# An order for every engine, laid out by the kernel itself, in a gated attention and bilinear feed-forward kernel

## The chip, the cores and the metric

The kernel runs on one core of a Trainium2 chip. The metric is the device time of one execution in microseconds (us); the times given are medians of several runs. A core has a matrix engine (PE, with its weight loads shown as PEld), a vector engine (DVE), an activation engine (ACT), GpSimd (POOL), and SP, whose queue issues all transfers of this kernel. The order in which an engine's instructions stand is fixed when the kernel is built; this case is about that order.

## The reference

```
for t in range(S):                       # B=4, H=8, S=768, D=40
    m_new = max(f_gate[t] + m, i_gate[t])
    f_stab = exp(f_gate[t] + m - m_new);  i_stab = exp(i_gate[t] - m_new);  m = m_new
    C = f_stab * C + i_stab * outer(v[t], k[t])
    n = f_stab * n + i_stab * k[t]
    h = C @ q[t];  denom = max(|n . q[t]|, 1)
    y[t] = sigmoid(o_gate[t]) * h / denom
x = y as [3072 tokens, 320]
out = ((x @ w_a) * (x @ w_b)) @ w_out     # w_a, w_b: 320 x 1536; w_out: 1536 x 320
```

All inputs are float32 but the three weights, which come as 64-bit numbers (an 11.8 MB load).

## The kernel before, in words

*Attention.* The recurrence is worked in chunks of 128 steps: 6 chunk rows c by 4 batches b make 24 chunks n, eight heads each. A chunk loads q and k (`qk`, three buffers) and v (`va`, three buffers), forms the masked decay matrix E from the gates (POOL L409, eight exponentials on ACT L416), the scores (`pS`, PE L471, in bf16 pieces that transposing transfers `T<-qks`, L448, have turned), their product with E split in three bf16 pieces (DVE L476, L480, L482, ACT L478), the products with v (`pV`, PE L523) and with the state carried over (`pI`, L497), the state's update (`pU`, L547, and `cst`, `cb`, which go through `c_dram`), and the end: the denominator, the sigmoid of the o gate (`squash`, L167), the products L610 and L613, a copy L615, the transposes `pX` (L633) and the split into a leading and a rest part, `xh` (ACT L637) and `xl` (DVE L639). The o gate of a chunk row has one buffer (`osig`), so its four loads wait for the chunk row before. The pieces q and k are split on DVE at L438 to L445. Chunks 0 to 5 use a plainer form (`begin_...`, L784 to L877).

*Feed-forward.* The 24 chunks are grouped in nine blocks of 2 or 3 (`sizes`). A block runs over twelve column groups ff of 128: two up products of eight matmuls each into `pu` (L747; three buffers in PSUM), then ACT or DVE copies one (`g`, L754), DVE multiplies (L755), a leading part `gh` (L757) and a rest `gl` (L759) are made, and two groups later the down products add into `pd` (L719; one buffer per chunk of the block). `xh` and `xl` have two buffers, so attention may be one block ahead.

*Weights.* They arrive in 32 stages (`fetch`, L331) and are converted once from 64-bit numbers: `high` (ACT L342), `low` (ACT L352), `join` (DVE L357), `lead_part` (ACT L370) and `low_part` (DVE L376).

*What sets the order.* Three means. The prologue (gates, chunks 0 and 1, stages 0 to 4) is written out by hand for PE, ACT, DVE and SP. From then on `run_block` walks a block's matmuls and between them pulls pieces of attention from a generator in a fixed proportion (a letter of `PATTERN` is a piece of a chunk). In blocks 0 and 1 the framework takes this as a priority and orders by its own estimate of time, held back by `issue_after`: nothing is issued ahead of the prologue's last instruction on its engine, and loads keep their order behind the weights. From block 2 on PE and SP keep the order as written, and the framework orders ACT, DVE and POOL:

```
    for kb in range(2):
        run_block(kb)
    with tc.manual_schedule(engines={mybir.EngineType.PE, mybir.EngineType.SP}):
        for kb in range(2, NB):
            run_block(kb)
```

Of the kernel before, what the change touches and what calls it, by code (L numbers as in the profile page):

```python
# [1 line left out]

# [14 lines left out]
PSUM = bass.MemoryType.PSUM  # L17


@with_exitstack  # L20
def kernel(
# [13 lines left out]
    nc = tc.nc  # L35
# [18 lines left out]
    rpool = ctx.enter_context(tc.tile_pool(name="rpool", bufs=1))  # L54
    apool = ctx.enter_context(tc.tile_pool(name="apool", bufs=2))
    dpool = ctx.enter_context(tc.tile_pool(name="dpool", bufs=1, space=bass.MemoryType.DRAM))
    ps_up = ctx.enter_context(tc.tile_pool(name="ps_up", bufs=3, space=PSUM))
    ps_dn = ctx.enter_context(tc.tile_pool(name="ps_dn", bufs=1, space=PSUM))
    ps_at = ctx.enter_context(tc.tile_pool(name="ps_at", bufs=2, space=PSUM))


    ident = wpool.tile([P, P], F32, name="ident")
    make_identity(nc, ident)
    NQ = 3
# [55 lines left out]
    after = {}  # L120
# [4 lines left out]
    issued = {}  # L125
# [12 lines left out]
    def load_qk(n, parts=(0, 1)):  # L138
        c, b = chunks[n]
        for j in parts:  # L140
            x = (q, k)[j]
            issued["qk"[j], n] = nc.sync.dma_start(
                nat(n)[0][:, j, :, 0:D], x[b, :, c * P:(c + 1) * P, :].rearrange("h t d -> t h d")
            ).ins

    def load_v(n):
        c, b = chunks[n]
        issued["v", n] = nc.sync.dma_start(
            nat(n)[1][:, :, 0:D], v[b, :, c * P:(c + 1) * P, :].rearrange("h t d -> t h d")
        ).ins  # L150

    def load(n):
        with tc.issue_after(issued.get(("v", n - 1), issued["w"])):
            load_qk(n)
            load_v(n)
# [9 lines left out]
    def squash(c, b, nb):  # L165
        x = osig[c][:, b:b + nb, 0:DM]
        after["s", c, b] = nc.scalar.activation(x, x, AF.Sigmoid).ins  # L167

    def load_o(c):
        for b in range(B):  # L170
            with tc.issue_after(issued["k", c]):
                fetch_o(c, b)
        squash(c, 0, B)

    def load_g(n):
# [4 lines left out]
        return nc.sync.dma_start(t, g_dram[c:c + 1, b * H:(b + 1) * H, :].broadcast_to([P, H, P])).ins  # L180
# [33 lines left out]
    def later_gates():  # L214
        f, i, m = (x[:, P:] for x in (gf, gi, gm))
        G = tab[0:BH]
        with tc.issue_after(start["dve"]):
            nc.vector.tensor_tensor_scan(m, f, i, gm[:, P - 1:P], op0=ALU.add, op1=ALU.max)
# [5 lines left out]
        with tc.issue_after(start["act"]):  # L224
            nc.scalar.copy(G[:, 0], gb3[0][:, 0])
            nc.scalar.copy(tab[BH:2 * BH, 0], gb3[0][:, 1])
# [7 lines left out]
        with tc.issue_after(issued["w"]):  # L234
            nc.sync.dma_start(g_dram.rearrange("c g t -> g c t"), G)
# [86 lines left out]
    def fetch(x):  # L322
# [6 lines left out]
        with tc.issue_after(issued.get("w", issued["k", 0])):  # L329
            for a in src:  # L330
                raw_in = nc.sync.dma_start(raw[r0:r0 + a.shape[0]], a).ins  # L331
                r0 += a.shape[0]
        issued["w"] = raw_in
# [32 lines left out]
    def lead_part(x):  # L366
        raw, n, W = held[x]
        w = ws[x] = rpool.tile([P, 2, n], F32R, tag=f"s{x}", name=f"w{x}")
        for rows, other, j, jl in parts(x):
            after["act"] = nc.scalar.copy(w[rows, j], W[rows]).ins  # L370

    def low_part(x):
        raw, n, W = held.pop(x)
        w = ws[x]
        for rows, other, j, jl in parts(x):
            after["dve"] = nc.vector.tensor_tensor(  # L376
                w[other, jl], W[rows], w[rows, j].bitcast(F32), op=ALU.subtract
            ).ins

    def weights():  # L380
        for x in range(NF0, len(stages) + 1):
            if x < len(stages):
                with tc.issue_after(start["act"]):
                    high(x)
                    low(x)
                with tc.issue_after(start["dve"]):
                    join(x)
# [206 lines left out]
    def stage_f(n):  # L594
# [10 lines left out]
        after["r", n] = nc.vector.reciprocal(den, den).ins  # L605
# [15 lines left out]
    def stage_d(n):  # L621
# [15 lines left out]
        after["h", n] = nc.scalar.copy(xh[:, :, cols], px).ins  # L637
        yield
        after["x", n] = nc.vector.tensor_tensor(  # L639
            xl[:, :, cols], px, xh[:, :, cols].bitcast(F32), op=ALU.subtract  # L640
        ).ins
# [6 lines left out]
    def aside(o, n):  # L648
        if o == "L" and n + 2 < NCH and n + 2 > NS + 1:
            with tc.issue_after(issued["w"]):  # L650
                load(n + 2)
# [52 lines left out]
    def moe_block(kb):  # L704
# [27 lines left out]
        def up(ff):  # L732
# [5 lines left out]
            for j in range(2):  # L738
# [7 lines left out]
                for x, (a, r) in enumerate(terms):  # L746
                    up_in = nc.tensor.matmul(  # L747
                        acc[j], a, r, start=(x == 0), stop=(x == len(terms) - 1),
                    ).ins
                    start.setdefault("pe", up_in)  # L750
# [21 lines left out]
    def begin_e(n):  # L772
# [5 lines left out]
        first_t = after["t"]  # L778
        for hf in range(2):
            pE = ps_up.tile([P, HH, P], F32, tag="pu", name=f"pE{n}_{hf}")  # L780
            for x in range(HH):
                one_hot = sel[:, b * H + hf * HH + x:b * H + hf * HH + x + 1].broadcast_to([3 * BH, P])
                with tc.issue_after(first_t):
                    nc.tensor.matmul(pE[:, x], one_hot, stk[:, 0], start=True, stop=False)  # L784
# [5 lines left out]
    def begin_a(n):  # L790
# [6 lines left out]
        for j in range(2):  # L797
# [9 lines left out]
            for x in range(HH):  # L807
                after["t"] = nc.tensor.transpose(
                    pt[:, x], nat(n)[0][:, j, 2 * x:2 * x + 2, :].rearrange("t h d -> t (h d)"), ident
                ).ins  # L810
# [71 lines left out]
    def lead(pieces, by):  # L882

        for _ in iter(int, 1):
            with tc.high_priority(by):
                x = next(pieces, "end")
# [5 lines left out]
    cpool = ctx.enter_context(tc.tile_pool(name="cpool", bufs=1))  # L892
    mpool = ctx.enter_context(tc.tile_pool(name="mpool", bufs=3))
# [5 lines left out]
    with tc.manual_schedule(engines={mybir.EngineType[x] for x in ("PE", "Activation", "DVE", "SP")}):  # L899
        fetch_gates(slice(0, P))  # L900
        load_qk(0)
        fetch(0)
        load_qk(1)
        load_v(0)
        fetch(2)
        load_v(1)
        fetch(4)
        fetch_o(0, 0)
        fetch(1)
        fetch_o(0, 1)  # L910
        fetch(3)
        fetch_gates(slice(P, S))
        for x in range(5, 13):
            fetch(x)
        load(2)
        for x in range(13, 16):
            fetch(x)
        for b in range(2, B):
            fetch_o(0, b)
        for x in range(16, 24):  # L920
            fetch(x)
        for x in range(24, len(stages)):
            fetch(x)

        idle = apool.tile([P, H * DV], F32, tag="vr", name="idle").bitcast(BF16)[:, 0:512]
        nc.vector.memset(idle, 0.0)
        warm = ps_dn.tile([P, 512], F32, tag="pd2", name="warm")
# [142 lines left out]
```

## Time and profile before

| | |
|---|---|
| median of 3 runs | 552.43 us (551.82 to 552.81) |
| the profiled execution's own time | 555.06 us |
| its span, first to last instruction | 553.3 us |
| instructions | 12427 |
| mean granted PE clock | 0.975 |
| HBM read, written | 41.11 MB, 5.97 MB |

The page gives busy time by engine and by line; a row such as "L747 PE MATMUL pu<-xh,w ... x1080 | 281.3, 327 | 2.1" is a line of the kernel, its engine, what it writes and reads, how many instructions, their busy time together, the mean duration of one in ns, and the engine's idle time ahead of them with what ended it. Matmuls overlap in PE, so their mean duration is not the pace at which they follow each other. A row by stretch gives the stretch, its length, the busy time of each engine with its instructions, the granted PE clock (1.00 is full), the share of time that the transfer engines were busy, and GB/s. A row of waits reads: engine, what waited, "<-", what it waited for, then us in total, times, and the longest.

### The profile page before, as it was taken

The page shows a single profiled execution, that of the slowest core. Times are in us where ns is not written, and L with a number is a line of the kernel's source. Part 1 is how long each engine was busy: PE and PEld are TensorE (multiplying, and loading weights), DVE is VectorE, ACT ScalarE, POOL GpSimd, SP SyncE. Part 2 cuts the span into 40 slices and gives each one's busy share as a digit, 9 for nine tenths or more (in the row PEclk, how much of TensorE's full clock was granted, in tenths as well). Part 3 has the DMA queues.
Part 4 walks back from the last instruction along what each step waited for, and adds up shares of the span by engine and source line. Part 5 has one row for each costly group of instructions (what it writes and reads, how often), then busy time and mean ns, then how long its engine had stood idle before and what let it go on. Part 6 is the DMA issues. An engine that isn't in the chain of part 4 may idle for free.

```text
span 553.3 us, 12427 instructions
## 1 busy us (share of the span) xinstructions
PE 529.7 (96%) x4810; PEld 504.1 (91%) x4810; DVE 407.9 (74%) x940; ACT 233.8 (42%) x559; POOL 126.5 (23%) x185
## 2 busy tenths in 40 slices
PE   9668999999999999999999999999999999899997
PEld 6568899998999999999899999899999999799997
DVE  6887868769799885997589895887777568744342
ACT  5699986434433451343342341542331514210111
POOL 2003534543143223133043122133030202100000
PEclk9687899999999999999999999999999999999999
DMA  9999814778639756569558564957555745100001
GB/s 174 307 253 318 146 28 101 161 139 154 109 97 186 153 95 129 107 110 188 92 130 163 117 113 122 157 104 155 84 130 78 134 77 131 21 1 25 1 0 37
DMA packets 198679, 66.77 MB, mean 121 GB/s; under 512 B 184252, under 2 KB 191900, under 8 KB 198620
## 3 DMA queue, kind: packets, MB, share of 16 engines
q1 hardware_dynamic: 198620, 65.98, 58.2%
q8 instruction: 38, 0.62, 0.5%
q14 instruction: 21, 0.17, 0.1%
HBM read 41.11 MB, written 5.97 MB: 85 GB/s over the span
## 4 chain that ended last, share of the span: by engine, by line
PE 74%; ACT 10%; DVE 5%; DMA 5%; issue 4%; SPq 2%; POOL 1%; POOLq 0%; ACTq 0%; DVEq 0%
PE pu L747 40%; PE pd L719 20%; PE pV L523 3%; DMA osig<-in_o_gate_dram 2%; PE pS L471 2%; PE pU L547 2%; ACT qks L342 1%; ACT L167 1%; ACT w L370 1%; PE pS L821 1%; PE pX L633 1%; PE pV L873 1%; SPq L160 1%; ACT cw L352 1%; ACT gbc L416 1%
## 5 line engine op out<-in xcount | busy, mean ns | idle before, releaser
L747 PE MATMUL pu<-xh,w 128*128 128x384 f32 (+1 forms) x1080 | 281.3, 327 | 2.1 <-ACT gbc L787 0.7
L747 PE MATMUL pu<-xl,w 128*128 128x384 f32 (+1 forms) x648 | 210.3, 326 | 1.0 <-DVE xl L639 1.0
L747 PEld LDWEIGHTS pu<-xh,w 128*128 128x128 f32 x1080 | 193.9, 192 | 4.0 <-ACT xh L637 1.0
L719 PE MATMUL pd<-w,gh 128*128 128x320 f32 x576 | 132.2, 316 | 2.8 <-ACT gh L757 2.8
L747 PEld LDWEIGHTS pu<-xl,w 128*128 128x128 f32 x648 | 124.6, 192 | 1.8 <-DVE xl L639 1.3
L719 PEld LDWEIGHTS pd<-w,gh 128*128 128x128 f32 x576 | 98.0, 191 | 3.5 <-ACT gh L757 3.2
L755 DVE TENSOR_TENSOR g<-pu,g 128x384 f32<-128x384 f32 (+1 forms) x108 | 54.7, 507 | 58.8 <-PE pu L747 55.5
L754 ACT COPY g<-pu 128x384 f32<-128x384 f32 (+1 forms) x92 | 40.4, 439 | 116.0 <-PE pu L747 114.7
L719 PE MATMUL pd<-w,gl 128*128 128x320 f32 x288 | 89.3, 319 | 0.0
L416 ACT ACTIVATE gbc<-gbc,gtab 128x128 f32<-128x128 f32 x160 | 49.2, 391 | 21.5 <-POOL gbc L409 19.8
L458 POOL TENSOR_TENSOR vr<-va 128x336 f32<-128x336 f32 x18 | 14.1, 782 | 188.7 <-PE pV L523 178.3
L719 PEld LDWEIGHTS pd<-w,gl 128*128 128x128 f32 x288 | 53.8, 191 | 0.2
L759 DVE TENSOR_TENSOR gl<-g,gh 128x384 fp32r<-128x384 f32 (+1 forms) x92 | 50.8, 552 | 1.6
L757 DVE CAST gh<-g 128x384 fp32r<-128x384 f32 (+1 forms) x96 | 34.2, 356 | 1.6
L478 ACT CAST pb<-gbc 128x512 bf16<-128x512 f32 x36 | 22.2, 616 | 29.4 <-DVE gbc L476 29.4
L530 DVE TENSOR_TENSOR num<-pV,num 128x336 f32<-128x336 f32 x18 | 9.1, 505 | 31.7 <-PE pV L523 31.6
L565 ACT CAST cb<-cst 128x168 bf16<-128x168 f32 x18 | 6.0, 332 | 54.5 <-DMA gbc<-g_dram 21.4
L610 POOL TENSOR_TENSOR osig<-osig,den 128x320 f32<-128x320 f32 x22 | 17.7, 804 | 41.1 <-DVE den L605 22.1
L409 POOL TENSOR_SCALAR_AFFINE_SELECT gbc<-gbc 128x1024 f32<-128x1024 f32 x20 | 23.6, 1182 | 14.6 <-DMA gbc<-g_dram 12.3
L476 DVE TENSOR_TENSOR gbc<-pS,gbc 128x512 f32<-128x512 f32 x36 | 24.5, 681 | 3.3 <-PE pS L471 3.3
L523 PEld LDWEIGHTS <-pb 128*128 128x128 bf16 x576 | 23.0, 96 | 4.1 <-DVE pb L482 1.8
L523 PE MATMUL pV<-va,pb 128*128 128x42 bf16 x288 | 25.0, 183 | 1.6 <-DVE pb L482 1.6
(131 smaller groups left out, 809.1 us busy)
## 6 DMA issues: line engine op xcount, KB each, us to landing
gbc<-g_dram SPq DMA_DIRECT2D x20, 512.0 KB
qk<-in_q_dram SPq DMA_DIRECT2D x24, 160.0 KB
qk<-in_k_dram SPq DMA_DIRECT2D x24, 160.0 KB
va<-in_v_dram SPq DMA_DIRECT2D x24, 160.0 KB
osig<-in_o_gate_dram SPq DMA_DIRECT2D x24, 160.0 KB
raw<-in_moe_w_out_dram SPq DMA_DIRECT2D x12, 320.0 KB
out_dram<-o SPq DMA_DIRECT2D x24, 160.0 KB
raw<-in_moe_w_a_dram SPq DMA_DIRECT2D x8, 384.0 KB
```

What stands on the lines that cost most here:

```text
L409: nc.gpsimd.affine_select(E, E, pattern=[[0, H], [1, P]], compare_op=ALU.is_ge, fill=-1e30, base=0, channel_multiplier=-1,)
L416: nc.scalar.activation(E[:, h], E[:, h], AF.Exp, bias=beta[:, h:h + 1])
L476: nc.vector.tensor_tensor(E, pS, E, op=ALU.mult)
L478: nc.scalar.copy(pb[:, 0], E)
L523: nc.tensor.matmul(pv[:, h], pb[i][:, h % HH, :], vb[j][:, h], start=(x == 0), stop=(x == len(terms) - 1),)
L610: (nc.vector if n < NS else nc.gpsimd).tensor_tensor(yv, yv, den.unsqueeze(2).broadcast_to([P, H, D]), op=ALU.mult)
L719: nc.tensor.matmul(pd[t][:, 0:DM], a[:, cols], w, start=(ff == 0 and first), stop=(ff == NF - 1 and last),)
L747: up_in = nc.tensor.matmul(acc[j], a, r, start=(x == 0), stop=(x == len(terms) - 1),).ins
L754: (nc.vector.tensor_copy if kb > 0 and ff in [1, 2] else nc.scalar.copy)(g, acc[0])
L755: nc.vector.tensor_tensor(g, acc[1], g, op=ALU.mult)
L757: (nc.vector.tensor_copy if kb > 0 else nc.scalar.copy)(gh, g)
L759: (nc.gpsimd if kb * 12 + ff < 16 else nc.vector).tensor_tensor(gl, g, gh.bitcast(F32), op=ALU.subtract)
```

## The change

The kernel no longer issues an instruction when the code reaches it. `nc` is now a recorder: each call is noted with the tiles it reads and writes (and the box within the tile, where it is known); up to eight matmuls in a row into the same tile make one node. Tiles come from pools that hand out stand-ins; the real tile is taken at the first use in the final order. From the notes the kernel makes edges: data dependencies, reuse of a ring's buffers, and the order in which a ring's tiles were first used. The instructions of the prologue keep their order on PE, ACT, DVE and SP (`pinned`); the transfers after the prologue's first ones do not. Each node has a time from a formula. The order is then made by passes in turn: a forward pass issues, at each engine, of the ready nodes the one of lowest rank (at first the recorded order); a backward pass over the same graph gives each node its latest begin, which is the next forward pass's rank. There are six turns, and the forward order with the earliest reckoned end is emitted, with every engine, POOL too, held to it. `issue_after` and `high_priority` are gone. One thing else changes: the sigmoids of the o gate for batches 2 and 3 of chunk row 0 become one instruction over both.

```
    def add(self, engine, op, args, kw):
...
        if not (
            eng == "PE" and node is not None and node.eng == "PE" and node.acc[0][0] == okey
            and len(node.calls) < 8 and node.pinned == self.pinned
        ):
            node = Node(len(self.nodes), eng)
...
    def cost(self, node, eng, op, out, refs, args, kw):
        cols = int(np.prod(out.shape[1:]))
        if eng == "PE":
            if op == "transpose":
                occ = 0.109
            else:
                if size[1] == 2:
                    occ = cols / 2400 + 0.005 if cols > 64 else 0.026
                elif "float32r" in f32[0]:
                    occ = cols / 2400 + 0.011
                else:
                    occ = 0.108 if refs[1].shape[0] <= 64 else 0.22
            node.occ += occ
            node.lat = 0.17
        elif eng == "ACT":
            node.table = "S" if "Sigmoid" in func else "E" if "Exp" in func else None
            node.occ = 0.04 + cols * 0.00094 + (0.13 if bias else 0.0)
            node.occ += 0.05 if "Prelu" in func or "scale" in kw else 0.0
            node.lat = 0.11
        elif eng == "DVE":
            rate = 960.0
            if one:                                  # copy, tensor_scalar, memset, no PSUM
                rate = 1920.0 if max(size) == 4 else 3840.0
            if op == "tensor_tensor_scan":
                rate = 480.0
            node.occ = 0.065 + cols / rate
            node.lat = 0.085
        elif eng == "POOL":
            node.occ = 0.1 + cols * (0.0009 if op in ("affine_select", "memset") else 0.002)
            node.lat = 0.1
        elif op == "dma_start_transpose":
            node.occ, node.lat, node.xfer = 1.3, 1.6, 0.0
        else:
            node.occ, node.lat = 0.47 if rows > 512 else 0.6, 1.7
            node.xfer = n / (390e3 if rows > 512 else 175e3)
...
    def link(self):
...
                    if key.first is None:
                        key.first = node
                        rings.setdefault(key.ring, []).append(key)
...
            if node.pinned:
                if node.eng in chain and node.eng != "POOL":
                    self.edge(chain[node.eng], node, order=True)
                chain[node.eng] = node
        for ring in rings.values():
            for a, b in zip(ring, ring[1:]):
                self.edge(a.first, b.first, order=True)
            for a, b in zip(ring, ring[ring[0].ring[2]:]):
                for k in a.users:
                    self.edge(k, b.first)
...
    def run(self, rank, forward=True):
...
            if x.table and x.table != table:
                table = x.table
                t += 1.283
...
    def settle(self):
        self.link()
        rank = [float(x.i) for x in self.nodes]
        best = None
        for turn in range(TURNS):
            order, at, end = self.run(rank)
            if best is None or end < best[1]:
                best = (order, end, at)
            back, late, _ = self.run([-t for t in at], forward=False)
            rank = [-(t + x.occ) for t, x in zip(late, self.nodes)]
        return best[0]
```

And in the kernel:

```
+    nc = plan
...
-            with tc.issue_after(issued["w"]):
-                load(n + 2)
+            load(n + 2)
...
+    plan.pinned = False
     for x in range(5, 13):
         fetch(x)
     load(2)
...
+    plan.pinned = True
...
     ready[0] = NF0
-    start = {x: after[x] for x in ("act", "dve")}
+    plan.pinned = False
...
-        for b in range(2, B):
-            squash(0, b, 1)
+        squash(0, NS, B - NS)
...
-    with tc.manual_schedule(engines={mybir.EngineType.PE, mybir.EngineType.SP}):
-        for kb in range(2, NB):
-            run_block(kb)
+    for kb in range(2, NB):
+        run_block(kb)
+
+    order = plan.settle()
+    with tc.manual_schedule():
+        plan.emit(order)
```

More of the change, by code (lines that the diff above doesn't have):

```diff
@@ L328, in fetch @@
         r0 = 0
[L329 to L333, printed above, removed]
+        for a in src:
+            nc.sync.dma_start(raw[r0:r0 + a.shape[0]], a)
+            r0 += a.shape[0]
         W = cpool.tile([P, WCH], F32, tag="cv", name="cw", bufs=CVB)[:, :n] if x < NF0 else None
@@ L382, in weights @@
             if x < len(stages):
[L383 to L387, printed above, removed]
+                high(x)
+                low(x)
+                join(x)
                 yield x
@@ L884, in lead @@
         for _ in iter(int, 1):
-            with tc.high_priority(by):
-                x = next(pieces, "end")
+            x = next(pieces, "end")
             if x == "end":
@@ new lines @@
+    fetch_gates(slice(0, P))
+    load_qk(0)
+    fetch(0)
+    load_qk(1)
+    load_v(0)
+    fetch(2)
+    load_v(1)
+    fetch(4)
+    fetch_o(0, 0)
+    fetch(1)
+    fetch_o(0, 1)
+    fetch(3)
+    fetch_gates(slice(P, S))
+    plan.pinned = False
+    for x in range(5, 13):
+        fetch(x)
+    load(2)
+    for x in range(13, 16):
+        fetch(x)
+    for b in range(2, B):
+        fetch_o(0, b)
+    for x in range(16, 24):
+        fetch(x)
+    for x in range(24, len(stages)):
+        fetch(x)
@@ new lines @@
+    X = [stage_d(n) for n in range(NS)]
+    first_gates()
+    run(A[0], 2)
+    high(0)
+    run(E[0], 2)
+    low(0)
+    join(0)
+    lead_part(0)
+    run(S_[0])
+    run(A[1])
+    run(S_[0], 2)
+    run(A[1])
+    low_part(0)
+    run(E[1], 2)
+    run(S_[1])
+    high(2)
+    low(2)
+    join(2)
+    lead_part(2)
+    run(V[0], 2)
+    squash(0, 0, 1)
+    run(S_[1], 2)
+    low_part(2)
+    run(V[0])
+    run(V[1], 2)
+    run(F[0])
+    high(4)
+    run(F[0])
+    low(4)
+    join(4)
@@ L994 @@
+    run(X[0])
+    lead_part(4)
+    squash(0, 1, 1)
+    run(V[1])
+    run(F[1])
+    run(X[0])
+    run(F[1])
+    run(X[1])
+    run(X[0])
+    low_part(4)
+    high(1)
+    run(X[1])
+    low(1)
+    join(1)
+    lead_part(1)
+    run(X[1], 2)
+    run(X[0])
+    low_part(1)
+    high(3)
+    low(3)
+    join(3)
+    lead_part(3)
+    low_part(3)
+    ready[0] = NF0
+    plan.pinned = False
+    for g in (*A, *E, *S_, *V, *F, *X):
+        assert next(g, "end") == "end"
     conv = weights()
```

425 lines of the change are left out of this document (288 added, 137 removed).

## The prediction

> **What bounds the kernel now.** I read the page's first part, then the busy time by stretch, then who PE waits for, and last ACT's timeline. The page first:
>
> ```profile
> span 553.3 us, 12427 instructions
> PE 529.7 (96%) x4810; PEld 504.1 (91%) x4810; DVE 407.9 (74%) x940; ACT 233.8 (42%) x559; POOL 126.5 (23%) x185
> ```
>
> PE has work for 529.7 of 553.3 us, so by this row at most 23.6 us of idle time can be ordered away; DVE is second at 74%. Where the idle time lies:
>
> ```profile
> core 0: us, PE busy (x) PEld busy (x) DVE busy (x) ACT busy (x) POOL busy (x), PEclk, DMA share, GB/s
> 0.00:20.00 20.00, 16.54 (x141) 12.91 (x141) 13.33 (x37) 11.87 (x21) 3.42 (x22) 0.93 1.01 210
> 20.00:40.00 20.00, 14.44 (x99) 12.90 (x99) 17.24 (x33) 16.59 (x34) 0.56 (x3) 0.73 1.01 279
> 40.00:60.00 20.00, 16.07 (x141) 14.63 (x140) 16.04 (x31) 19.91 (x48) 6.36 (x9) 0.83 0.97 264
> 60.00:80.00 20.00, 19.67 (x151) 18.38 (x152) 14.21 (x29) 19.27 (x53) 7.65 (x10) 0.83 0.48 94
> 80.00:100.00 20.00, 20.00 (x155) 18.74 (x154) 17.73 (x38) 12.06 (x35) 11.42 (x19) 1.00 0.51 101
> 100.00:470.00 370.00, 365.50 (x3550) 350.05 (x3549) 293.14 (x691) 142.20 (x344) 95.69 (x121) 1.00 0.65 126
> 470.00:484.00 14.00, 11.52 (x158) 10.83 (x155) 10.72 (x29) 3.15 (x7) 1.44 (x2) 1.00 0.12 24
> 484.00:553.30 69.30, 65.96 (x429) 65.69 (x427) 25.53 (x56) 8.79 (x20) 0.00 (x0) 1.00 0.04 13
> ```
>
> PE's idle time is 3.5 us before 20, 9.5 us from 20 to 60, 0.3 us to 80, 4.5 us over the 370 us to 470, 2.5 us from 470 to 484, and 3.3 us in the last stretch. There are four stages. To 20 us inputs arrive (DMA share 1.01). From 20 to 80 ACT is the bound: 16.59, 19.91 and 19.27 busy of 20 each, while PE idles and its granted clock is 0.73 to 0.83. From 80 to 484 PE is the bound. In the last stretch only the last block's two products and the way out are left; PE has no other work there, so nothing can be reordered into it.
>
> ```profile
> PE pX L633 <- DVE osig L613: 5.4, 5, 2.7
> PE pd L719 <- ACT gh L757: 2.8, 2, 1.7
> PE pT L808 <- DMA qk<-in_q_dram: 2.5, 1, 2.5
> PE pV L523 <- DVE pb L482: 1.6, 2, 0.9
> ```
>
> PE's waits are few and short: these four groups are 12.3 us in ten waits. They are heads of a queue in program order that wait for a vector engine although other products are in the queue behind them. Such waits another order can fill.
>
> [...]
>
> **The change part by part.**
>
> *What stays.* No matmul, vector operation or transfer is added, and only one goes: two sigmoids of 128x320 (o gate, batches 2 and 3 of the first chunk row) become one of 128x640. The order of tiles in each ring is kept, so up, down and attention products each keep their own order on PE, and only their merging changes. The kernel before also ran fixed orders, written by hand for PE and SP from block 2 on, and by the framework for the rest. So the change costs no time of its own, and what it gives is read from the stretches.
>
> *ACT from 26 to 89 us.* The weights' conversion is bound to ACT:
>
> ```profile
> 25.80:88.90 63.10, 58.42 (x141) 0.85 0.76 184
> L342 ACT ACTIVATE qks<-raw 128x384 f32<-128x384 f32 (+1 forms) x32 | 17.4, 545 | 0.1
> L352 ACT ACTIVATE cw<-raw 128x384 uint32<-128x384 uint32 (+1 forms) x27 | 14.0, 532 | 0.0
> L370 ACT CAST w<-cw 128x384 fp32r<-128x384 f32 (+2 forms) x36 | 18.1, 503 | 7.1 <-DVE cw L357 6.9
> 33.18 1.28 ACT L787 ACT_TABLE_LOAD   x1
> 35.09 1.28 ACT L167 ACT_TABLE_LOAD   x1
> 36.87 1.28 ACT L787 ACT_TABLE_LOAD   x1
> 39.64 1.28 ACT L167 ACT_TABLE_LOAD   x1
> 49.73 1.28 ACT L263 ACT_TABLE_LOAD   x1
> ```
>
> (The first row is ACT alone over that stretch.) The three conversion groups, 49.5 us in all, mostly lie here, and no order makes them shorter. The five table loads are 6.4 us in ACT's bound stretch: exponential, sigmoid, exponential, sigmoid, exponential. With one sigmoid left for both batches at least one pair, sigmoid and back, falls away: 2 x 1.28 = 2.6 us. If the sigmoid goes ahead of every exponential, four loads fall away (5.1 us); if the order stays as alternating as now through other pieces, none. I take 2.6, ends 0 and 5.1.
>
> *The start edges.* Before, conversions and attention had to be issued behind the last prologue instruction of ACT, DVE and PE; these edges are gone, and the prologue alone stays chained. From 20 to 40 us ACT is idle for 20 - 16.59 = 3.4 us, most of it as the hand order's copies wait for DVE; conversions of stages already landed can go there. I take half, 1.7, ends 0 and 3.4. Since ACT is the bound until 80, both terms move everything behind them.
>
> *SP.* The transfers of weight stages 5 to 31 (30), chunk 2's q, k, v (3) and two of the o gate (2) are unpinned: 35 transfers whose places the planner sets. To 60 us the DMA share is 0.97 to 1.01, so the order decides who is late and not how much is moved. Chunk 2's 480 KB ahead of the weights, or behind them, is 480 / 279 = 1.7 us either way; I take 0, ends -1.7 and +1.7. The planner counts long rows at 390 bytes per ns, and the stretch shows 279: for 11.8 MB of weights 30 us against 42, so it thinks them 12 us early at the end. What covers this:
>
> ```profile
> L342 ACT ACTIVATE qks<-raw x32: 487/556/597, 7.1 to 79.7; 128x384 f32<-128x384 f32 x20, 128x320 f32<-128x320 f32 x12
> L331 SPq DMA_DIRECT2D raw<-in_moe_w_out_dram x12: 328/430/1636, 14.9 to 48.3; - x12
> ```
>
> The last weight transfer is issued at 48.3 and first touched by ACT's last conversion at 79.7: 31 us of slack. Without that cover the cost would be up to 12 us.
>
> *The steady stretch, 100 to 470 us.* 4.5 us of idle PE. The planner begins a product as soon as it reckons its inputs there and puts up or down products ahead until then; the three buffers of the up results and two sets of x limit how far. I take half, 2.2, ends 0 and 4.5. What is late next are the o gate's loads, once in four chunks, which one set of buffers keeps behind the chunk before.
>
> *The end of the attention, 470 to 484 us.*
>
> ```profile
> 472.33 0.56 PE L471 MATMUL pS<-T,T 120*128 120x128 bf16 x7 [0.36 <-DMA T<-qks]
> 479.00 0.22 PE L523 MATMUL pV<-va,pb 128*128 128x42 bf16 x2 [0.69 <-DVE pb L482]
> 482.32 0.52 PE L633 MATMUL pX<-ident,osig 128*128 128x128 f32 x3 [1.42 <-DVE osig L613]
> ```
>
> The last chunk is finished with block 7 already used up: 0.36 + 0.69 + 1.42 = 2.5 us, PE's whole idle time there. A rank by latest begin, worked back from the end, holds block 7's products for these gaps, or has the chunk done earlier. I take all 2.5, ends 0 and 2.5.
>
> *POOL* gets a fixed order too. It is 23% busy; I cost that at nothing, covered by its idle time, and with that gone one piece of the attention would be late by one POOL operation, which the rival below includes in kind.
>
> **Sum:** 2.6 + 1.7 + 0 + 2.2 + 2.5 = 9.0 us. The profiled execution took 555.06 us (span 553.3 and 1.8 around it), 0.5% over the median of 552.43; taken off the median, 9.0 us leave 543.4.
>
> **The rivals.**
>
> *The clock comes back too.* From 20 to 80 us the granted clock is 0.73, 0.83, 0.83: 5.4 + 3.4 + 3.4 = 12.2 us of half-rate time lost. If the planner fills the whole 9.5 us of idle PE from 20 to 60 instead of 4.3, and half of the 12.2 comes back since PE no longer pauses, the time is 543.4 - 5.2 - 6.1 = 532. For it: the low clock lies only where PE idles, and from 80 us on the row says 1.00. Against: ACT, not PE, is the bound there, and a faster PE would wait for it. [...]
>
> *No slack in the plan: slower.* Place: 80 to 484 us. The planner's durations of DVE's attention operations are too short, so a product put on PE just as its input is reckoned there stops PE:
>
> ```profile
> L438 DVE TENSOR_TENSOR r<-qk,qks 128x320 f32<-128x320 f32 x36 | 24.3, 674 | 0.0
> L444 DVE COPY qks<-qks 128x640 bf16<-128x640 bf16 x36 | 14.7, 407 | 0.1
> L482 DVE TENSOR_TENSOR pb<-gbc 128x512 bf16<-128x512 f32 x36 | 25.1, 697 | 0.0
> L613 DVE TENSOR_TENSOR osig<-num,osig 128x320 f32<-128x320 f32 x20 | 13.9, 698 | 1.6 <-POOL osig L610 1.2
> L615 DVE COPY osig<-osig 128x64 f32<-128x64 f32 x18 | 7.9, 440 | 0.0
> ```
>
> By the formula in the diff (0.065 us, elements by a rate, and 0.085 us to be seen) they are 0.483, 0.317, 0.683, 0.483 and 0.183 us. So L438 is short by 0.19 and L444 by 0.09, both twice a chunk, L613 by 0.21 and L615 by 0.26: 1.03 us a chunk, 18.6 us over 18 late chunks. It decides from the point where 9.0 / 18.6, about half, reaches PE; at four fifths, 14.9 us, the time is 558. For it: the misses stand right ahead of the transposes on which PE already waits longest (L613). Against: L482, the largest, is right to 0.014, and DVE has 20% of idle time there to catch up in.
>
> *The change does not do what it says.* With every ring's order kept, the merge may come out as the hand's, and ACT's tables as before: 552.
>
> **How the numbers follow.** Forecast 0.48, clock rival 0.22, slower 0.22, no change 0.08. The forecast's own range, from its terms' ends, is 537 (all: 15.5 us) to 552 (none). The whole range takes in both rivals: low 530 (9.5 and 7.0 us of idle time and 6.1 of clock off 552.4), high 558. About 0.2% (1.1 us) can be told from no change here. Faster is the forecast and the clock rival, 0.70; slower 0.22; same 0.08.
>
> **What would show it.** Right: three table loads or fewer between 26 and 89 us, ACT's conversions done before 86, idle PE of 470 to 484 gone, the pX wait for L613 under 2 us in all. Wrong: waits of PE for pX, pS or pV in tens from 80 to 484 (slower); granted clock over 0.9 from 20 to 80 (clock rival); conversions of ACT waiting for raw (the weights' slack was not there).

## The result, and the profile after

The changed kernel takes 558.01 us (median of 5 runs, 556.23 to 558.91) against 552.81 us (551.82 to 554.03) for the kernel before: a ratio of 1.0087, with a 95% interval of 1.0061 to 1.0113. It is slower by 5.2 us; 543.4 had been forecast. The profiled execution has a span of 556.2 us, against 553.3; that of the kernel before took 555.06 us, 2.3 over its median, so the rows below show less of the loss than the 5.2 us.

In the trace of the changed kernel every instruction carries one line, L341, the place where the plan is emitted, so its rows are read by their tiles. The page's first part:

```profile
span 556.2 us, 12412 instructions
PE 527.8 (95%) x4810; PEld 505.7 (91%) x4810; DVE 408.6 (73%) x940; ACT 234.6 (42%) x556; POOL 125.8 (23%) x185
```

No engine has over 2 us more to do than before. So the busy time by stretch is next; the columns are those of the prediction's table. First the kernel before, put together in three stretches:

```profile
core 0: us, PE busy (x) PEld busy (x) DVE busy (x) ACT busy (x) POOL busy (x), PEclk, DMA share, GB/s
0.00:80.00 80.00, 66.72 (x531) 58.81 (x532) 60.83 (x127) 67.64 (x154) 17.99 (x44) 0.83 0.87 212
80.00:140.00 60.00, 58.74 (x548) 55.80 (x547) 48.15 (x109) 29.68 (x80) 29.81 (x42) 1.00 0.67 131
140.00:484.00 344.00, 338.28 (x3308) 323.83 (x3307) 273.44 (x649) 127.73 (x307) 78.75 (x100) 1.00 0.62 119
```

and the kernel after in the same three, with the last 14 us of the attention once more by themselves:

```profile
0.00:80.00 80.00, 57.81 (x476) 50.70 (x477) 56.56 (x121) 56.99 (x128) 15.93 (x41) 0.81 0.90 208
80.00:140.00 60.00, 57.95 (x472) 56.29 (x471) 41.92 (x95) 33.67 (x89) 26.21 (x37) 0.89 0.53 108
140.00:484.00 344.00, 343.18 (x3377) 330.21 (x3376) 281.17 (x660) 133.87 (x318) 82.91 (x106) 1.00 0.62 124
470.00:484.00 14.00, 14.00 (x182) 13.72 (x181) 13.39 (x35) 5.60 (x15) 0.72 (x1) 1.00 0.50 77
```

From 140 to 484 us PE's idle time falls from 5.7 to 0.8 us, and from 470 to 484 nothing of it is left: what the prediction wanted there came. To 80 us it rises from 80 - 66.72 = 13.3 to 80 - 57.81 = 22.2 us, and from 80 to 140 the clock that was 1.00 is now 0.89. The gain is late and the loss is early. How they add up is seen by following the down products, tile `pd`: the twelve column groups of a block of two chunks hold 72 of them, so the 72nd ends block 0 and the 144th ends block 1. These are the rows of `pd` alone (PE, PEld, ACT), cut at those two places, before and then after:

```profile
0.00:100.90 100.90, 17.73 (x72) 12.92 (x72) 0.00 (x0) 0.86 0.79 188
100.90:151.80 50.90, 13.75 (x72) 10.85 (x72) 1.13 (x3) 1.00 0.73 140
151.80:553.30 401.50, 125.10 (x721) 109.78 (x720) 8.99 (x22) 1.00 0.52 101
```

```profile
0.00:104.50 104.50, 14.85 (x72) 10.93 (x72) 0.31 (x1) 0.85 0.77 174
104.50:160.10 55.60, 15.19 (x73) 12.25 (x72) 0.96 (x3) 0.88 0.68 136
160.10:556.30 396.20, 125.08 (x720) 109.66 (x720) 8.77 (x22) 1.00 0.51 103
```

Block 1 ends 8.3 us later (160.1 against 151.8), and all behind it takes 5.3 us less (396.2 against 401.5): 2.9 us of span lost between these two profiled executions. PE's longest waits over the whole span all lie in the early stretch and name three places (us in total, times, longest):

```profile
PE pT L341 <- DMA qk<-in_k_dram: 9.6, 1, 9.6
PE pX L341 <- DVE osig L341: 6.5, 2, 6.1
...
PE pI L341 <- DVE gbc L341: 2.1, 1, 2.1
```

**The long one.** At 62.95 us PE goes on with the transposes of chunk 3's k, after 9.62 us with nothing else at the head of its queue. SP's timeline and PE's (start, duration, operation, in brackets the idle time before it) show where that load had been:

```profile
25.68 5.19 SPq L341 DMA_DIRECT2D osig<-in_o_gate_dram  x2
...
48.64 2.28 SPq L341 DMA_DIRECT2D raw<-in_moe_w_out_dram  x3
...
53.84 0.38 SPq L341 DMA_DIRECT2D qk<-in_q_dram  x1
...
56.95 3.17 SPq L341 DMA_DIRECT2D qk<-in_k_dram  x1
```

```profile
62.95 0.90 PE L341 MATMUL pT<-ident,qk 128*128 128x128 f32 x3 [9.62 <-DMA qk<-in_k_dram]
```

The load of k stands behind all weights in SP's queue. In the plan's own reckoning (the times that the kernel's formulas give when it is built) the last weight is issued at 28 us and this load at 39, when its buffer is free, to land at 51.3; on the chip they are issued at 50.6 and 56.95. SP did not get through its queue as fast as reckoned: in the first row two issues take 5.19 us, where the six single ones ahead of it take 0.43 to 0.67 each, and from 20 to 58 us SP's waits, 11.0 us in all, are for transfers alone. The plan has these transposes at 51.4, right behind the landing that it reckons, and leaves PE idle for the 4.4 us ahead of them. So it did not think the load long done: it gave it no slack, and reckoned a wait for it, only a shorter one. In the kernel before, the order on SP is much the same and a k lands at about the same time:

```profile
46.51 2.13 SPq L331 DMA_DIRECT2D raw<-in_moe_w_out_dram  x3
...
56.72 0.68 SPq L142 DMA_DIRECT2D qk<-in_k_dram  x1
```

```profile
61.54 0.66 PE L808 MATMUL pT<-ident,qk 128*128 128x128 f32 x4 [0.16 <-DMA qk<-in_k_dram]
```

but there PE does block 0's up products until it is in, and waits 0.16 us. The load is not late because of the change; the instruction that needs it has been put 11.6 us too early.

Another transfer behind the weights stands at POOL's head. The store of the gate tables, `g_dram<-qks`, is issued at 28 us in the plan and at 51.70 on the chip, and POOL, now held to an order too, waits 8.0 us for it; DVE then waits for POOL, and ACT for DVE:

```profile
60.42 0.23 POOL L341 MEMSET qks<- 128x64 bf16 x2 [8.00 <-DMA g_dram<-qks]
61.14 0.33 DVE L341 TENSOR_TENSOR cst<-cst,dec 128x168 f32<-128x168 f32 x1 [4.27 <-POOL cr L341]
61.98 0.51 ACT L341 CAST w<-cw 128x384 fp32r<-128x384 f32 x1 [3.53 <-DVE cw L341]
```

```profile
60.00:80.00 20.00, 17.05 (x112) 16.40 (x113) 11.79 (x25) 12.99 (x31) 5.82 (x9) 0.68 0.54 88
```

ACT, busy for 19.27 us from 60 to 80 in the kernel before, is busy for 12.99. The loss does not hang on that: in e1_rate below ACT is busy for 19.26 of the same 20 us, and the time is no shorter.

**The short one.** The product `osig`, ahead of the first transposes `pX`, is late because the plan let the decay sums of the later chunks into DVE's prologue, which the start edges had kept out. On DVE:

```profile
19.99 1.54 DVE L341 TENSOR_TENSOR_SCAN qks<-qks 32x640 f32<-32x640 f32 x1 [0.43 <-DMA qks<-in_i_gate_dram]
...
25.00 0.49 DVE L341 TENSOR_TENSOR osig<-pV,osig 128x320 f32<-128x320 f32 x1
```

The first up product starts at 27.1 us instead of 22.2. Here too the plan itself reckons idle time, 5.1 us ahead of the `pX` of 21.4 us.

**The clock.** The stretches at clock 0.50 in the first 140 us, those of the changed kernel first, then the first and the last of four in the kernel before:

```profile
18.30:31.90 13.60, 5.99 (x25) 5.24 (x26) 12.54 (x27) 8.05 (x20) 0.09 (x1) 0.50 1.09 276
55.80:72.90 17.10, 9.96 (x56) 9.57 (x57) 8.71 (x18) 9.64 (x22) 4.21 (x7) 0.50 0.86 152
120.67:134.33 13.66, 13.31 (x64) 13.01 (x65) 8.90 (x25) 4.21 (x13) 6.90 (x9) 0.50 0.86 158
```

```profile
17.20:27.40 10.20, 5.90 (x23) 4.86 (x24) 7.93 (x18) 6.24 (x16) 0.00 (x0) 0.50 1.10 313
...
65.00:71.80 6.80, 6.80 (x40) 6.38 (x41) 5.98 (x14) 6.61 (x21) 3.97 (x5) 0.50 0.56 90
```

Together they are 44.4 us against 27.2 (10.2, 3.4, 6.8 and 6.8), with PE busy for 29.3 and 22.2 us of them. The second stretch of the changed kernel lies around the wait for k, the third behind the wait of 2.1 us of `pI`.

### The profile page after: what moved, and what is told of

It is laid out like the page before. It is cut to its first block, busy times and chain, and to the rows that moved or that the text cites. A ratio compares the mean times of both kernels' runs of the same rounds, so it can differ in the third digit from the quotient of the medians.

```text
span 556.2 us, 12412 instructions
## 1 busy us (share of the span) xinstructions
PE 527.8 (95%) x4810; PEld 505.7 (91%) x4810; DVE 408.6 (73%) x940; ACT 234.6 (42%) x556; POOL 125.8 (23%) x185
## 4 chain that ended last, share of the span: by engine, by line
PE 84%; DMA 8%; SPq 4%; DVE 2%; issue 1%; ACT 0%; POOL 0%; DVEq 0%; POOLq 0%; ACTq 0%
PE pu L341 47%; PE pd L341 22%; PE pV L341 6%; SPq L341 4%; PE pS L341 4%; PE pI L341 2%; DMA raw<-in_moe_w_a_dram 2%; PE pU L341 2%; DMA raw<-in_moe_w_out_dram 1%; PE pX L341 1%; DMA raw<-in_moe_w_b_dram 1%; DMA qk<-in_k_dram 1%; DMA qks<-in_f_gate_dram 1%; DVE qks L341 1%; DMA va<-in_v_dram 1%
## 5 line engine op out<-in xcount | busy, mean ns | idle before, releaser
L341 PE MATMUL pu<-xh,w 128*128 128x384 f32 (+1 forms) x1080 | 279.1, 326 | 0.0
L341 PE MATMUL pu<-xl,w 128*128 128x384 f32 (+1 forms) x648 | 210.3, 327 | 1.1 <-DVE xl L341 1.1
L341 PEld LDWEIGHTS pu<-xh,w 128*128 128x128 f32 x1080 | 193.5, 192 | 0.7
L341 PE MATMUL pd<-w,gh 128*128 128x320 f32 x576 | 135.2, 316 | 0.4 <-DVE w L341 0.3
L341 PEld LDWEIGHTS pu<-xl,w 128*128 128x128 f32 x648 | 124.5, 192 | 2.1 <-DVE xl L341 1.4
L341 PEld LDWEIGHTS pd<-w,gh 128*128 128x128 f32 x576 | 98.3, 190 | 1.1 <-DVE w L341 0.5
L341 DVE TENSOR_TENSOR g<-pu,g 128x384 f32<-128x384 f32 (+1 forms) x108 | 54.5, 505 | 54.6 <-PE pu L341 52.7
L341 PE MATMUL pd<-w,gl 128*128 128x320 f32 x288 | 90.8, 316 | 0.3 <-POOL gl L341 0.3
L341 ACT COPY g<-pu 128x384 f32<-128x384 f32 (+1 forms) x92 | 40.2, 437 | 97.1 <-PE pu L341 96.8
L341 POOL TENSOR_TENSOR vr<-va 128x336 f32<-128x336 f32 x18 | 14.8, 824 | 221.1 <-PE pV L341 220.0
L341 ACT ACTIVATE gbc<-gbc,gtab 128x128 f32<-128x128 f32 x160 | 54.2, 393 | 18.2 <-POOL gbc L341 18.1
L341 PEld LDWEIGHTS pd<-w,gl 128*128 128x128 f32 x288 | 54.5, 189 | 0.8 <-POOL gl L341 0.6
L341 DVE TENSOR_TENSOR gl<-g,gh 128x384 fp32r<-128x384 f32 (+1 forms) x92 | 51.2, 557 | 2.1
L341 ACT CAST pb<-gbc 128x512 bf16<-128x512 f32 x36 | 22.3, 619 | 47.7 <-DVE gbc L341 47.5
L341 PE MATMUL pV<-va,gbc 128*128 128x42 bf16 (+1 forms) x240 | 36.9, 238 | 0.0
L341 DVE CAST gh<-g 128x384 fp32r<-128x384 f32 (+1 forms) x96 | 33.3, 346 | 1.8
L341 DVE TENSOR_TENSOR gbc<-pS,gbc 128x512 f32<-128x512 f32 x48 | 32.4, 679 | 1.8 <-PE pS L341 1.4
L341 DVE TENSOR_TENSOR num<-pV,num 128x336 f32<-128x336 f32 x20 | 10.1, 504 | 31.4 <-PE pV L341 31.4
L341 ACT CAST cb<-cst 128x168 bf16<-128x168 f32 x18 | 6.0, 332 | 60.5 <-DVE cst L341 39.4
L341 PEld LDWEIGHTS <-T 120*128 120x128 bf16 x576 | 24.7, 97 | 6.5 <-issue 4.4
L341 PE MATMUL pS<-T,T 120*128 120x128 bf16 (+1 forms) x352 | 29.6, 236 | 0.0
L341 ACT CAST qks<-qk 128x320 bf16<-128x320 f32 x36 | 16.1, 454 | 29.9 <-DMA T<-qks 25.3
```

The lines of the kernel that those rows point to most:

```text
L341: f(*[real(x) for x in args], **{k: real(x) for k, x in kw.items()})
```

## The experiments

The reading to be tested: the order costs time because the plan reckons transfers issued too early and puts what needs them at PE's head. The rivals: the freed start edges crowd the early engines; the planner's ranking by latest begin is itself bad (a rank from a graph with wrong durations); or DVE's durations are too short. The table gives all twelve, each against runs of the kernel before beside it (medians 552.44 to 553.0): median, ratio and interval, the end of block 1, PE's idle time and mean granted clock over the first 140 us. From block 1's end to the end of the span it is 395.4 to 397.8 us in every kernel with the plan (400.8 in e6_squash, 401.5 before), so only the early stretch tells them apart.

| | us | ratio [95%] | block 1 ends | PE idle to 140 | clock to 140 |
|---|---|---|---|---|---|
| before | 552.81 | | 151.8 | 14.6 | 0.90 |
| after | 558.01 | 1.0087 [1.0061, 1.0113] | 160.1 | 24.2 | 0.84 |
| e1_rate | 560.08 | 1.0138 [1.0109, 1.0166] | 161.9 | 23.7 | 0.84 |
| e5_block | 547.63 | 0.9904 [0.9865, 0.9944] | 151.5 | 15.4 | 0.88 |
| e3_rate_block | 545.39 | 0.9892 [0.9846, 0.9938] | 146.7 | 15.8 | 0.91 |
| e2_edges | 558.42 | 1.0113 [1.0083, 1.0144] | 159.1 | 20.8 | 0.87 |
| e7_edges_too | 553.16 | 1.0006 [0.9980, 1.0032] | 154.7 | 16.7 | 0.89 |
| e4_first | 558.89 | 1.0105 [1.0069, 1.0140] | 159.3 | 23.3 | 0.84 |
| e12_first_held | 561.47 | 1.0165 [1.0138, 1.0192] | 159.4 | 25.1 | 0.85 |
| e9_k3 | 556.93 | 1.0084 [1.0057, 1.0110] | 158.2 | 21.7 | 0.85 |
| e8_dve | 551.89 | 0.9988 [0.9957, 1.0018] | 154.8 | 15.5 | 0.84 |
| e10_scan | 551.59 | 0.9982 [0.9958, 1.0006] | 153.5 | 14.5 | 0.87 |
| e11_pool | 549.64 | 0.9920 [0.9883, 0.9958] | 153.6 | 14.5 | 0.88 |
| e6_squash | 553.12 | 1.0007 [0.9978, 1.0036] | 150.5 | 14.6 | 0.91 |

### The transfers: e1_rate, e5_block, e3_rate_block, e9_k3

The rate of long rows alone, as the trace shows it:

```
-                node.xfer = n / (390e3 if rows > 512 else 175e3)
+                node.xfer = n / (300e3 if rows > 512 else 175e3)
```

> The changed kernel with one number of the planner changed: long rows move at 300 bytes per ns instead of 390. Theory A (the planner puts PE work ahead of transfers that land later than it reckons): the 9.6 us wait of PE for chunk 3's k shrinks to under 4 us, and with it the half-rate stretch behind it; 6 to 10 us faster than the changed kernel, about 549. Theory B (the damage is the gate scans that the freed start edges let into DVE's prologue): the wait at 25 us and the late first up product stay, about 557. Theory C (late loads matter, but because SP's queue is full and not because of the rate): the wait stays at 8 us or more, about 557.

560.08 us, no gain. The wait for k stays, 8.5 us instead of 9.6:

```profile
PE pT L341 <- DMA qk<-in_k_dram: 8.5, 1, 8.5
```

With this rate the plan has the load landing at 60.5 us and the transposes at 60.6 (62.62 on the chip), with 12.4 us of idle PE ahead of them, and its own end at 540.1 us, where the changed kernel's plan ends at 530.7. So it sees the wait and cannot avoid it: weights wait for no buffer, and SP has issued them all by 28 us, before the buffer of k is free at 40.5. The rate is not what was wrong with the plan, or not alone. What the formula lacks is that SP did not run ahead of the transfers (the two issues of 5.19 us, the 11.0 us of waits): it lets an issue cost 0.47 us, and queues without limit. One line in the forward pass holds SP while more than 6 us of transfers are outstanding, here with the rate of 390 kept:

```
                     end[i] = wire + 0.35 if x.xfer else t + x.occ + x.lat
+                    free[e] = max(free[e], wire - 6.0)
```

> The changed kernel with the hold on SP alone (an issue waits while over 6 us of transfers are reckoned under way), long rows back at 390 bytes per ns. If the planner's error is the order in which a full queue lets transfers out, this alone gives what both gave: within 2 us of the run with rate and hold, 545. If the hold works only with a wire as slow as the real one (at 390 the backlog seldom reaches 6 us), the wait for chunk 3's k stays above 4 us and the time is 553 to 558.

547.63 us: this one line is worth 10.4 us against the changed kernel's 558.01, and makes the plan faster than the kernel before. What it changes is the place in SP's queue: when the buffer of k is free, SP still has weights to issue, and by its rank the load goes ahead of them (46.61 us, the last weights from 56.40). The plan's times are still too early, with k landing at 44.9 by its reckoning, ahead of its issue on the chip. So it is the order of the loads that counts here, more than the time reckoned for them. With both edits:

> As the first (300 bytes per ns), and the planner's SP holds an issue while more than 6 us of transfers are reckoned to be under way. Theory C: only here does the wait for chunk 3's k go, 8 us or more faster than the changed kernel, about 549, and at least 4 us faster than the run with the rate alone. Theory A: equal to the run with the rate alone within 2 us. Theory B: 557.

545.39 us (544.94 to 550.02), by its median the fastest kernel of this study, 1.1% faster than the one before (interval 0.6% to 1.5%). Its runs and those of e5_block (544.90 to 549.69) overlap, so a gain of the rate on top of the hold is not shown. In its SP queue two loads of k now stand among the weights, the last of which come behind them, and no wait for a transfer is left among PE's longest:

```profile
45.37 0.38 SPq L342 DMA_DIRECT2D qk<-in_k_dram  x1
50.18 0.38 SPq L342 DMA_DIRECT2D qk<-in_k_dram  x1
53.66 2.25 SPq L342 DMA_DIRECT2D raw<-in_moe_w_out_dram  x3
```

```profile
PE pX L342 <- DVE osig L342: 4.6, 1, 4.6
...
PE pI L342 <- DVE gbc L342: 1.9, 1, 1.9
```

To 80 us PE is idle for 13.1 us instead of 22.2, where the kernel before had 13.3:

```profile
0.00:80.00 80.00, 66.95 (x566) 59.02 (x567) 64.00 (x137) 64.69 (x148) 17.53 (x43) 0.89 0.91 212
```

Is it this one load, or the model? The changed kernel, with only chunk 3's k reckoned 20 us later:

```
+            if (n, j) == (3, 1):
+                plan.nodes[-1].lat += 20.0
```

> The changed kernel (390 bytes per ns, no hold), with 20 us added to the planner's landing time of one transfer, the k of chunk 3; the order is laid out anew. If that one transfer's lateness makes most of the loss, the 9.6 us wait is gone, block 1 ends 7 to 10 us earlier (150 to 153 us), and the time is 547 to 550. If other late transfers take its place at the head of PE's queue, another wait on a transfer of 4 us or more appears and the time stays at 555 to 559.

556.93 us, which these runs do not tell from after. The wait of 9.6 us is halved, and as long a one stands elsewhere:

```profile
PE ptg L341 <- DVE qks L341: 9.7, 1, 9.7
PE pT L341 <- DMA qk<-in_k_dram: 4.6, 1, 4.6
```

The plan reckons idle PE ahead of both, 7.7 and 5.5 us, and the load is still issued behind the last weights (55.00 us on the chip, those from 48.02). Mending one estimate only shifts the wait; the model of the queue had to be mended.

### The start edges: e2_edges, e7_edges_too

Every node behind the prologue gets an edge from the last prologue instruction of its engine (PE, ACT, DVE), as in the kernel before; first in the changed kernel, then with rate and hold:

```
                 chain[node.eng] = node
+            elif node.eng in ("PE", "ACT", "DVE"):
+                free.append(node)
+        for node in free:
+            self.edge(chain[node.eng], node, order=True)
```

> The changed kernel with the start edges put back: on PE, ACT and DVE every instruction behind the prologue is ordered after the prologue's last one. Theory B: the first up product is back at 22 to 23 us instead of 27.1, the 6.1 us wait of pX is gone, 4 to 6 us faster than the changed kernel, about 553. Theory A: the wait for chunk 3's k stays at about 9 us and eats what came earlier; under 2 us faster, about 557.

> Rate and hold, and the start edges put back. If the gate scans in DVE's prologue cost what PE waits there, the 4.6 us wait of pX goes, the first up product is back before 23 us, and the run is 3 to 5 us faster than the one with rate and hold, 541. If that work is only moved behind the prologue and the conversions wait for it there, the time is within 1.5 us of it, 545; and if DVE's and ACT's idle time in the prologue was of use, it is slower, 547 or more.

558.42 and 553.16 us. Without the hold the edges change nothing that can be told (558.01 after): the `pX` wait falls to 2.7, the wait for k stays at 5.8, and another of 4.2 comes in:

```profile
PE pT L345 <- DMA qk<-in_k_dram: 5.8, 1, 5.8
PE pS L345 <- DVE T L345: 4.2, 1, 4.2
```

With rate and hold they cost 7.8 us (553.16 against 545.39). So crowding by the freed edges is not the cause; freeing them is a gain, but one that is to be had only where SP is held.

### The ranking: e4_first, e12_first_held

One forward pass in the recorded order and no ranking by latest begin (`TURNS = 1` instead of 6), first in the changed kernel, then with rate and hold:

> The changed kernel with one turn instead of six: the first forward pass, ranked by the recorded order, is emitted, so no latest begin has a part in it. If the rank by latest begin makes the steady stretch dense, that stretch loses here: idle PE of 100 to 470 us goes from 2.9 back to 4 or more, 3 to 6 us slower than the changed kernel, about 562. If any forward pass that fills gaps does it, the steady stretch stays and the time is within 2 us of the changed kernel, about 557.

> Rate and hold, with one turn instead of six: the forward pass ranked by the recorded order, no latest begin. If the rank by latest begin gives something once the transfers are reckoned rightly, this is slower than rate and hold by 4 us or more, 549 to 554, by waits in the first 150 us or by idle PE between 140 and 484 us. If filling gaps in the recorded order is all that gains, it is within 2 us, 543 to 547, with the last stretch from block 1's end again about 393 us.

558.89 and 561.47 us. In the changed kernel the ranking gains 0.9 us, which these intervals do not tell from nothing, with rate and hold 16.1. The plan's own ends say the same: 530.7 us either way in the changed kernel, 528.6 against 537.6 with rate and hold. The hold without the ranking is no cure: in the recorded order the load of k goes behind all weights again (52.84 us on the chip, the last weights from 46.64), and PE waits for `pX`, `pV` and a load of q.

```profile
PE pX L342 <- DVE osig L342: 5.9, 3, 5.0
PE pV L342 <- ACT T L342: 5.7, 1, 5.7
PE pT L342 <- DMA qk<-in_q_dram: 3.4, 1, 3.4
```

The two runs also say something of the gain from 140 to 484: with one greedy pass by reckoned times PE is busy for 341.99 and 342.01 of these 344 us, 2.0 idle, where the kernel before had 5.7 and the changed kernel 0.8. So 3.7 of the 4.9 us come from merging by reckoned readiness, and the rest from the ranking.

### DVE's durations and two single waits: e8_dve, e10_scan, e11_pool

All three start from e3_rate_block. e8_dve raises DVE's copies to the durations that the traces show (`rate = 1200.0 if max(size) == 4 else 2000.0`):

> Rate and hold, and the planner's DVE copies made slower (elements by 1200 instead of 1920, and by 2000 instead of 3840 in 16 bits; 320 and 640 elements then take 0.42 and 0.47 us with the time to be seen, about what the trace of before shows). Theory D (the pause at 107 to 110 us, after which PE runs at half clock from 113 to 120, comes from DVE copies that take longer than reckoned): the wait of pI goes under 0.8 us, no half-clock stretch between 90 and 480 us, 3 to 5 us faster than with rate and hold, 541. Rival (the pause comes from POOL or from the early chunks' form): it stays, 545.

551.89 us, 6.5 us more than e3_rate_block. The `pI` wait at which it aimed stays at 1.9 us. DVE's durations are not what is missing. That they made a worse plan is not shown either: the plan's own end is 528.8 us against 528.6, and what differs is the clock, 0.960 to 0.969 over whole executions in its four runs against 0.978 in three of e3_rate_block's four; whether the plan brings that about is open.

e10_scan keeps the scan of the later chunks behind DVE's prologue (one edge from its last instruction):

> Rate and hold, and one instruction more held: DVE's scan over the later gates (640 elements, 1.5 us) is ordered behind DVE's last prologue instruction; ACT's and PE's freed edges stay. If the gate work in DVE's prologue makes PE wait for osig, the 4.6 us wait goes to under 3 us as in the kernel before, and the time is 2 to 4 us below the run with rate and hold, 542. If the early stretch is bound by ACT and the transfers anyway, block 1 ends within 1.5 us of that run and the time is 544 to 547. If the gate tables are then late for chunk 4, it is 548 or more.

551.59 us. The `pX` wait falls from 4.6 to 2.7 and the first up product comes at 23.3 us instead of 25.1, as it should; then `pS` waits 3.4 us for DVE, and block 1 ends 6.8 us later.

e11_pool takes two kinds of work off POOL that lie beside DVE's copies ahead of `pI`: the split's subtraction of the first chunks is on DVE throughout, and `gl` is on POOL for the first 12 column groups instead of 16:

> Rate and hold, with POOL relieved around 105 us: the last split of q and k of chunks 6 and 7 and four of the gl subtractions of block 1 go to DVE. If the pause at 107 to 110 us comes from DVE copies that run slowly beside POOL (0.73 us each there), the copies are near 0.33 us, the wait of pI and the half-clock stretch behind it go, and the time is 2 to 4 us below rate and hold, 542. If it comes from the chain POOL mask, ACT exponentials, DVE product itself, the wait stays at 1.5 us or more and the time is 544 to 548.

549.64 us (546.05 to 553.04). Its ten runs fall apart: four take 546.05 to 546.74 us at a mean clock of 0.977 to 0.978, like three of e3_rate_block's four, and six 548.87 to 553.04 at 0.966 to 0.972, the profiled one (551.41) among them. So it is not shown that this edit costs anything. The copies of 640 elements are shorter, 0.62 us for three against 2.92 us for four:

```profile
105.40 2.92 DVE L342 COPY qks<-qks 128x640 bf16<-128x640 bf16 x4
```

```profile
111.59 0.62 DVE L342 COPY qks<-qks 128x640 bf16<-128x640 bf16 x3
```

```profile
PE pI L342 <- DVE gbc L342: 2.9, 2, 2.0
```

and `pI` waits 2.0 us all the same. The copies are not what it waits for; that leaves the chain of that chunk (POOL's mask, ACT's exponentials, DVE's product), which no run shows to be it.

### The merged sigmoid alone: e6_squash

The kernel before with the one other edit of the change:

```
-        for b in range(2, B):
-            squash(0, b, 1)
+        squash(0, NS, B - NS)
```

> The kernel before, with only the two late sigmoids of chunk row 0 made one. The prediction's term says two table loads fall away on a bound ACT: 2.6 us faster than the kernel before, 550. If ACT's order around it, and not the table loads, decides when the conversions end, the time is within 1 us of the kernel before, 552.5. If the one sigmoid, which needs both batches' o gate, comes later than the first of two, chunk 2 is later and the time is 1 to 2 us longer.

553.12 us, the same within 0.4%. Three table loads instead of five, as forecast (they start at 32.88, 36.32 and 46.58 us), and not visible in the time. Block 1 ends 1.3 us earlier in the one profiled execution (150.5 against 151.8).

### What stays open

Among the kernels with the hold, PE's idle time to 140 us is nearly one (14.5 to 16.7, e12_first_held apart), yet block 1 ends anywhere from 146.7 to 154.8. The granted clock goes some way with it: 0.91 in the best and 0.84 in e8_dve, which over 140 us is at most 9.8 us of full-rate time. But e7_edges_too (0.89, 154.7) and e11_pool (0.88, 153.6) do not fit such a line, and nothing here set the clock by itself. Over whole executions the clock tells more: the span times its mean granted clock is 529.5 to 533.0 us in every run of e3_rate_block, e5_block, e8_dve, e10_scan and e11_pool, so these five differ in the clock and in little else, as e11_pool's own runs do among themselves. What decides the clock among these plans, whose edits are small, is not settled, nor what lies behind the `pI` wait of about 2 us that each of them has. The runs show that the queue's model is worth 10 to 13 us in this kernel, not that the last 3 to 5 us of e3_rate_block would survive another edit: e11_pool's own runs lie between 546 and 553 us.

## Why the prediction was wrong, point by point

- *SP, 0 with ends of 1.7 us: the step that failed.* It put the order of the 35 freed transfers at nothing. It noted that the planner would think the weights 12 us early, and let 31 us of slack between the last weight's issue and its first use cover it. That slack was there: no conversion's wait for a weight is among the longest of the trace. But the weights are not alone in the queue. The loads of q, k and v stand behind them, are reckoned too early as well, and k had no slack: it was reckoned to land at 51.3 us, was issued only at 56.95, and PE waited 9.6 us. With SP's hold the same planner's order is 10.4 us faster (e5_block), with the rate too 12.6 (e3_rate_block). The size of the misjudged time was seen; who else depends on it, and that an SP that is never held issues all weights ahead of these loads, was not asked. The rate named there was the lesser half: alone it gained nothing (e1_rate). A hint was on the table: of the four longest waits of PE, said to be for a vector engine, the third is for a load of q. The range left SP's own ends of 1.7 us out, too; with them it is 535 to 554.
- *POOL, nothing.* Its idle time did not cover it. Held to an order, it waited 8.0 us for a transfer behind the weights, not one POOL operation, and passed 4.3 us on to DVE and 3.5 to ACT. What that cost by itself no run shows; e1_rate, where ACT is not held up, is no faster.
- *Start edges, -1.7.* With the plan's transfers as they were, nothing (558.42 with them, 558.01 without). With rate and hold, freeing them saves 7.8 us. The direction was right under a condition that the change did not meet.
- *Table loads, -2.6.* The count came out as said, three. Alone it gave +0.7 us with an interval from -1.2 to +2.0 (e6_squash: -0.22% to +0.36% of 552.4), so 2.6 is excluded: two saved loads on ACT do not move the time by their length, though ACT is at 16.59 to 19.91 busy of 20 us. "Since ACT is the bound until 80, both terms move everything behind them" was too much: in e1_rate ACT is as busy from 40 to 80 us as before (19.20 and 19.26), and block 1 ends 10.1 us later. In the changed kernel the conversions end later, not sooner: the last `lead_part` starts at 93.8 us, where under 86 was forecast.
- *Steady stretch and end of attention, -2.2 and -2.5.* Right, and a little small: behind block 1 the plan saves 5.3 us where 4.7 had been said, idle time from 140 to 484 falls by 4.9, and from 470 to 484 to 0.00.
- *The rival of a faster clock (532).* It went the other way: 0.81 over the first 80 us against 0.83, and 0.89 from 80 to 140 against 1.00. That PE's pauses and the low clock go together fits the loss (PE idle for 24.2 us to 140 against 14.6, and 44.4 us at half clock against 27.2), but "only where PE idles" was too much: from 65.00 to 71.80 us in the kernel before PE is busy for all 6.80 us at clock 0.50. That half of the 12.2 us comes back as PE stops pausing was the author's estimate, and no run shows it: none has PE idle for less than 14.5 us to 140, and the two that have this (e10_scan and e11_pool) show clocks of 0.87 and 0.88, where the kernel before shows 0.90 with 14.6.
- *The slower rival (558).* The time is nearly its time by luck, since the mechanism is another. It put the misses on DVE from 80 to 484 us; there PE lost 2.9 us of 404 against 7.0 before, and longer DVE durations in the plan gained nothing (e8_dve). The misses were on SP, ahead of 80 us.
- *What would show it.* "Conversions of ACT waiting for raw" was the only sign named for a wrong reckoning of transfers; it did not come, and the loads of attention, where it showed, were not on the list. Of the wait for `osig`, under 2 us in all was forecast, and it is 6.5.

## What to carry to other kernels

A fixed order laid out by reckoned times is as good as its model of what all engines share; here the hold on SP while over 6 us of transfers are reckoned outstanding, which decides what may still go ahead of what, gained 10.4 us (e5_block) where the durations tried gained nothing (e1_rate, e8_dve), and the ranking by latest begin paid only with it (16.1 us against 0.9). In this order, held on every engine, a head that waited held up what stood behind it (PE 9.62 us for one load; POOL's 8.00 became 4.27 on DVE and 3.53 on ACT): before trusting the slack of one user of a shared queue, list who else stands behind it, and look at the first thing each needs. Fixing one late estimate moves the wait; fix the rule that put the load behind. And look for idle time in the plan itself: the two longest waits of PE stood there already, only shorter.

## What the hardware showed that was not expected

The granted clock fell to 0.50 at the end of a pause of 2.1 us and stayed there for 13.66 us. The changed kernel, by PE's granted clock around the 2.1 us wait of `pI`, which ends at 121.02 us (columns as above):

```profile
117.25:120.67 3.42, 1.72 (x26) 1.46 (x24) 2.96 (x6) 1.86 (x7) 2.28 (x4) 1.00 0.05 10
120.67:134.33 13.66, 13.31 (x64) 13.01 (x65) 8.90 (x25) 4.21 (x13) 6.90 (x9) 0.50 0.86 158
```

A stretch of 3.42 us with PE busy for half of it is followed by 13.66 us at clock 0.50, four times as long, with PE busy for 13.31 of them. If the pause of 2.1 us set it off, it took up to 6.7 us more (an estimate: half of 13.31, by the clock of 0.50). In e3_rate_block the same wait, 1.9 us, is followed by only 6.8 us:

```profile
112.90:119.70 6.80, 6.80 (x33) 6.80 (x33) 5.49 (x15) 2.23 (x6) 2.30 (x4) 0.50 1.04 165
```

and in the kernel before, a stretch with PE busy for 2.23 of 3.40 us is followed by no drop, its clock staying at 1.00 to the end of the attention:

```profile
351.60:355.00 3.40, 2.23 (x13) 1.75 (x12) 2.87 (x9) 2.41 (x5) 0.72 (x1) 1.00 0.92 170
```

The stretches at 0.50 in the three kernels are near multiples of 3.4 us (3.4, 6.8, 10.2, 13.6, 13.66, 13.70 and 17.1). What ends the slow stretch no run here shows.
